# Loads of later tokens and of the first gate-up weights issued behind named stores of packed queries and keys

## The chip, the core and the metric

The kernel runs on one core of a Trainium2 chip. TensorE multiplies matrices, VectorE (DVE in the profile), ScalarE (ACT) and GpSimd (POOL) work on tiles, and SyncE (SP) does nothing here but issue DMA transfers. The transfers that SyncE issues go into one queue, whose packets are spread over 16 DMA engines. The metric is the device time of one execution in microseconds; of several runs the median counts.

## What is computed

A layer norm of 2048 tokens of width 448 feeds two branches, and both are added to the input. One is causal attention with 16 heads of width 28 inside four blocks of 512 tokens, with a memory of the earlier blocks. The other is a gated feed-forward network with 1792 hidden columns.

```python
xn = _layernorm(x, axis=-1)
# attention, per block s of 512 tokens, 16 heads
logits = einsum("bhqd,bhkd->bhqk", qs, ks) * scale + mask
a_dot  = einsum("bhqk,bhkd->bhqd", softmax(logits), vs)
a_mem  = einsum("bhld,bhde->bhle", phi(qs), M) / (einsum("bhld,bhd->bhl", phi(qs), z)[..., None] + 1e-6)
o = g * a_mem + (1 - g) * a_dot          # g = sigmoid(beta)
M, z = M + phi(ks)^T vs, z + sum(phi(ks))
# feed-forward
h = sigmoid(xn @ w_gate) * (xn @ w_up)
return x + concat(o) @ wo + h @ w_down
```

## The kernel before

Every float32 operand of a large product is split into a high part and a low rest, and a product is a sum of eleven matmuls over the four slices of 128 rows that the width needs (the list TERMS).

The kernel has two stages. The front stage goes over the four blocks of 512 tokens. For block b it multiplies the values (`values`, L326 to L332), then runs a loop over seven packed tiles c of keys and queries, 128 columns each (`keys_queries`, L339 to L358). The keys fill the first 448 of the 896 packed columns and the queries the rest. Position k in the loop is c in the first three blocks. For each tile:

- TensorE makes pp (L344, eleven matmuls of 128x512).
- ScalarE copies it to the high half of the tile qk (L345), and makes e, the feature map of keys or queries, where it is needed (L349, L350).
- VectorE writes the low half of qk (L351).
- SyncE stores qk to the DRAM tensor qd, 512 KB (L352). For the queries of the second to fourth block it also stores e to the DRAM tensor fd (L357).

Between these, `key_rows` (L364, matmul pk, and the copy kn, L366) turns the keys of tile k - 2, and `update` (L372, matmul pmm) adds to the memory. `turn` (L95, matmul pt) turns the next block's normalised tokens into its operand. In a block after the second, `recall` (L390, matmul n) multiplies the memory with phi, which is read back from fd (`phi_queries`, L383).

The second stage runs the feed-forward network (`gated`) with attention in between, and then the output projection. TensorE is in its written order there too. The generator `ffn = gated()` is advanced a step at a time: its first step only calls `load_up(0)` (L178, a raw gate-up tile of 512 KB), and its second splits that tile (`ready_up(0)`), loads the next (`load_up(1)`, L178) and the first down tile (`load_down(0)`, L185, 224 KB). In the front stage these two steps are taken at k = 5 of the second and third block (L554). The further steps come in the last block.

What sets the order: in the front stage, TensorE, ScalarE and VectorE run their instructions in the order in which the program writes them. SyncE and GpSimd do not: the compiler's scheduler puts their instructions where it expects them to be ready. A load that depends on nothing can therefore stand far ahead of its place in the program. In before the loads of the third and fourth block's tokens (L528, tiles acc2 and acc3, 896 KB each), both raw gate-up tiles (L178) and the first down tile (L185) stand at the top of SyncE's queue, right behind the four small gate loads; only the store vd of the values (L332, 1024 KB) comes between. The first store of qk comes behind all of them.

The tag "4k" of the pool `mid` has four buffers. At the start two hold wv's raw halves and one holds the last raw tile of wqk. The tile qk of c = 0 takes the fourth, c = 1 and c = 2 take wv's, c = 3 takes the buffer of c = 0 once its store has landed, and c = 4 that of wqk's raw tile.

PSUM banks are shared likewise: pk of odd c and pmm of even i use one bank with the tag "pd", so the first pmm waits until the copy kn has emptied the second pk.

Of the kernel before, what the change touches and what calls it, by code (L numbers as in the profile page):

```python
# [9 lines left out]
F32 = mybir.dt.float32  # L10
# [6 lines left out]
P = 128  # L17
# [44 lines left out]
def kernel(  # L62
# [10 lines left out]
    nc = tc.nc  # L73
# [8 lines left out]
    acc = [keep.tile([P, NT, D], F32, name=f"acc{b}") for b in range(NB)]  # L82
# [25 lines left out]
    def x_block(b):  # L108
        return x[b * L:(b + 1) * L, :].rearrange("(t p) d -> p t d", p=P)
# [5 lines left out]
    def bank(name, tag):  # L115
        return ps.tile([P, L], F32, name=name, tag=tag, bufs=banks[tag])
# [17 lines left out]
    qd = [dram.tile([2 * D, 2, L], F32, name=f"qd{b}") for b in range(NB)]  # L134
# [9 lines left out]
    def four_k(dtype, name):  # L144
        return mid.tile([P, 2, L], dtype, name=name, tag="4k", bufs=4)
# [122 lines left out]
    with tc.tile_pool(name="front", bufs=2) as sb, tc.manual_schedule(engines=FRONT):  # L268
# [10 lines left out]
        def statistics(b, t0, steps):  # L279

            stats = sb.tile([P, steps, 6], F32, name=f"stats{steps}")
            mv = sb.tile([P, steps, 2], F32, name=f"mv{steps}")
            vh = sb.tile([P, steps], F32, name=f"vh{steps}")
            for t in range(steps):
                V.bn_stats(stats[:, t, :], acc[b][:, t0 + t, :])  # L285
                V.bn_aggr(mv[:, t, :], stats[:, t, :])
            V.tensor_scalar(vh, mv[:, :, 1], EPS, -0.5, op0=ALU.add, op1=ALU.mult)
            return mv, vh

        def root(vh):  # L290
            y = sb.tile([P, vh.shape[1]], F32, name=f"y{vh.shape[1]}")
            A.activation(y, vh, AF.Sqrt, scale=-2.0)
            return y
# [15 lines left out]
        def normalise(b, t, mean, y):  # L309
            xn = sb.tile([P, 512], F32, name="xn")  # L310
            V.tensor_scalar(xn[:, :D].rearrange("p (m h c) -> p h m c", h=H, c=4),
                              acc[b][:, t, :].rearrange("p (h m c) -> p h m c", h=H, c=4), mean, y,
                              op0=ALU.subtract, op1=ALU.mult)
            if b == 0:
                A.activation(xn[:, D:], xn[:, 384:D], AF.Copy)
            else:
                G.tensor_copy(xn[:, D:], xn[:, 384:D])
            return xn

        def turn(b, t, xn):  # L320
            transpose_split(bank("pt", "s"), xn, xs[b], t)
# [7 lines left out]
        def store_values(b, t, pv):  # L329
            A.activation(vst[:, t, :, :DH], pv[:, :D].rearrange("p (h d) -> p h d", d=DH), AF.Copy)  # L330
            if t == NT - 1:
                nc.sync.dma_start(vd[b], vst.rearrange("p t h d -> p t (h d)"))  # L332

        def values(b, t):
            pv = bank("pv", "p")
            value_terms(b, t, pv, EARLY[1] if b == 0 else TERMS)
            store_values(b, t, pv)

        def keys_queries(b, c):  # L339

            qk = four_k(F32R, "qk")
            pp = bank("pp", ("p", "gu" if b < NB - 1 else "s")[c % 2])
            for n, (a, w) in enumerate(TERMS):
                T.matmul(pp, wqk[c][:, w, :], xs[b][:, a, :], start=n == 0, stop=n == len(TERMS) - 1)  # L344
            A.activation(qk[:, 0, :], pp, AF.Copy)  # L345
            e = None
            if (c < 4 and b < NB - 1) or (c > 2 and b > 0):
                e = sb.tile([P, L], F32, name="e", tag="e", bufs=5)
                A.activation(e, pp, AF.Relu, scale=-1.0)  # L349
                A.activation(e, e, AF.Exp, scale=-1.0)  # L350
            V.tensor_sub(qk[:, 1, :], pp, qk[:, 0, :].bitcast(F32))  # L351
            nc.sync.dma_start(qd[b][c * P:(c + 1) * P], qk.bitcast(F32))  # L352
            if e is not None:
                V.scalar_tensor_tensor(e, pp, 0.0, e, op0=ALU.max, op1=ALU.add)
                if c > 2 and b > 0:
                    lo = max(c * P - D, 0)
                    nc.sync.dma_start(fd[b][lo:(c + 1) * P - D], e[D + lo - c * P:])  # L357
            return e  # L358
# [22 lines left out]
        def phi_queries(b, i):  # L381
            phi = sb.tile([GW, L], F32, name="phi", tag="e", bufs=5)
            nc.sync.dma_start(phi, fd[b][i * GW:(i + 1) * GW])  # L383
            return phi

        def recall(b, i, phi):
            ts = sb.tile([P, L], F32, name="ts", bufs=1)
            tb = sb.tile([P, L], F32, name="tb", bufs=2)
            n2 = bank("n2", ("m", "pd")[i % 2])
            T.matmul(n2, mst[b % 2][i], phi, start=True, stop=True)  # L390
            V.transpose(ts, n2)
            weigh(sb, ts, gate[:, i:i + 1], MEM_EPS)
            V.transpose(tb, ts)
            nc.gpsimd.dma_start(od[b][P * i:P * (i + 1)], tb)
# [28 lines left out]
        def split_qk(c):  # L423
            r = raw_qk[c].rearrange("p (c n) -> p c n", c=4)
            A.activation(wqk[c][:, 0:4, :], r, AF.Copy)
            G.tensor_sub(wqk[c][:, 4:8, :], r, wqk[c][:, 0:4, :].bitcast(F32))
# [65 lines left out]
        ffn = gated()  # L492
        for b in range(NB):
            last = b == NB - 1
            phi, xn = {}, {}
            if b > 1:
                phi = {i: phi_queries(b - 1, i) for i in range(NG)}
            st = None
            for t in range(3 if b == 0 else 0, NT):
                values(b, t)  # L500
                if b > 1 and t > 0:
                    recall(b - 1, t - 1, phi[t - 1])
                if b == 0:
                    split_qk(t)
                if last:
                    continue
                if t == (3 if b == 0 else 0):
                    mv, vh = statistics(b + 1, 0, NT)
                if t == (3 if b == 0 else 0):
                    st = mv, vh, root(vh)  # L510
                if t == (3 if b == 0 else 2):
                    A.activation(one, ident[:, 0:1], AF.Exp)  # L512
            if st and b > 0:
                st = rstd(*st)
                for n in range(2):
                    xn[n] = normalise(b + 1, n, *st[n])
            e = {}
            for k, c in enumerate((3, 4, 5, 6, 0, 1, 2) if last else range(7)):
                e[c] = keys_queries(b, c)
                if b == 0 and c + 4 < 7:  # L520
                    split_qk(c + 4)
                if k == 0:
                    if b > 1:
                        recall(b - 1, NG - 1, phi[NG - 1])
                    if b == 0:
                        st = rstd(*st)
                    if b < 2:
                        nc.sync.dma_start(acc[b + 2], x_block(b + 2))  # L528
                    if b == 0:
                        A.activation(gate, gate, AF.Exp, scale=-1.0)  # L530
                        V.tensor_scalar_add(gate, gate, 1.0)
                        V.reciprocal(gate, gate)
                        V.tensor_scalar(gate_n, gate, -1.0, 1.0, op0=ALU.mult, op1=ALU.add)
                if last:
                    if k > 0:
                        next(ffn)
                    if 2 <= k < 6:
                        phi[k - 2] = phi_queries(b, k - 2)
                    if k > 4:
                        begin[k - 5]()  # L540
                        recall(b, k - 5, phi[k - 5])
                    continue
                if 2 <= k < 6:
                    key_rows(k - 2, e[k - 2])
                if 4 <= k:
                    update(b, k - 4)
                if k == 6:
                    update(b, 3)
                n = k - 1 if b == 0 else k + 1
                if 2 <= n < 6:  # L550
                    turn(b + 1, n - 2, xn[n - 2])
                if 0 <= n < 4 and n not in xn:
                    xn[n] = normalise(b + 1, n, *st[n])
                if b in (1, 2) and k == 5:  # L554
                    next(ffn)
            if last:
                for i in range(2):
                    for _ in range(FILLS[i]):
                        next(ffn)
                    if i == 0:  # L560
                        begin[2]()
                    recall(b, i + 2, phi[i + 2])
# [207 lines left out]
    with tc.manual_schedule(engines=MANUAL):  # L770
        next(steps)
        k = sum(FILLS) + 6
# [46 lines left out]
```

## Time and profile before

| what | value |
|---|---|
| three runs | 696.43, 697.25, 699.18 us |
| median | 697.25 us |
| span of the profiled execution | 697.6 us |
| DMA packets | 45797, 84.37 MB |
| mean granted TensorE clock | 0.997 of full |

The profiled execution is one execution of its own, and its span goes from its first to its last instruction; the profile gives no other time for it.

How to read it: a row of the timeline gives start and length in us from the span's start, the engine, the line of the program, the work as output <- inputs, how many instructions are merged, and in brackets the idle time of the engine before it with what ended it. A "q" behind an engine's name is its instruction queue, which issues DMAs. PEld is the weight load of a matmul, which overlaps the matmul before it. A row of the windows gives, for one stretch, the busy time of each engine and, as its last three numbers, the granted TensorE clock, the mean busy share of the DMA engines, and GB/s. A piece of the chain that reads "DMA qd<-qk" goes from the issue of a store to its landing.

### The profile page before, as it was taken

Reading aid. Unit: us, or ns where it says so; the run is one execution under the profiler, and the core shown is the slowest. Engines: PE = TensorE matmul, PEld = TensorE weight load, DVE = VectorE, ACT = ScalarE, POOL = GpSimd, SP = SyncE. Lnnn points to the kernel's source line nnn. Section 1 sums busy time; section 2 is a strip of 40 time slices with the busy share of each in tenths; the row PEclk is TensorE's granted clock in tenths of the full one; section 3 lists DMA queues with packets and bytes.
Section 4 is the critical chain, followed back from the end, with each engine's and each line's share of the span. In section 5 each row is a group of like instructions: output and inputs, shape, how many; then the busy total and the mean of one; then the engine's idle time right before and its main releaser. Section 6 shows DMA issues by size and latency. Waiting matters only on the chain.

```text
span 697.6 us, 10438 instructions
## 1 busy us (share of the span) xinstructions
PE 690.0 (99%) x3594; PEld 567.7 (81%) x3594; DVE 570.2 (82%) x994; ACT 343.6 (49%) x563; POOL 148.5 (21%) x349
## 2 busy tenths in 40 slices
PE   8989999999999999999999999999999999999997
PEld 7878878777878787877878778787787878778897
DVE  6665687658789898988898889998898889889863
ACT  5646646344455455543655446455644555446320
POOL 4400010101222131322222222132221322222000
PEclk9999999999999999999999999999999999999999
DMA  7833545687222423234323343324242432333342
GB/s 265 320 130 149 201 185 211 226 300 224 70 77 65 120 86 85 48 113 108 78 58 96 70 128 66 98 56 114 74 108 66 95 70 60 86 94 88 91 152 105
DMA packets 45797, 84.37 MB, mean 121 GB/s; under 512 B 6321, under 2 KB 20401, under 8 KB 45233
## 3 DMA queue, kind: packets, MB, share of 16 engines
q1 hardware_dynamic: 42736, 76.37, 35.3%
q0 software_dynamic: 3008, 7.34, 5.2%
q8 instruction: 28, 0.46, 0.3%
q14 instruction: 25, 0.20, 0.1%
HBM read 51.05 MB, written 32.64 MB: 120 GB/s over the span
## 4 chain that ended last, share of the span: by engine, by line
PE 94%; DMA 2%; DVE 1%; ACT 1%; SPq 0%; issue 0%; ACTq 0%
PE pgu L240 42%; PE pd L166 20%; PE pp L344 9%; PE st L597 5%; PE pa L672 5%; PE po L756 5%; PE pv L326 4%; PE pmm L372 2%; PE n L390 1%; DMA qd<-qk 1%; DMA acc<-in_x 1%; PE pt L95 1%; PE pk L364 1%; DVE stats L285 0%; ACT L512 0%
## 5 line engine op out<-in xcount | busy, mean ns | idle before, releaser
L240 PE MATMUL pgu<-xs,wgu 128*128 128x512 f32 x1232 | 321.0, 398 | 0.0
L240 PEld LDWEIGHTS pgu<-xs,wgu 128*128 128x128 f32 x1232 | 226.6, 188 | 48.0 <-issue 3.2
L166 PE MATMUL pd<-wdn,hh 128*128 128x448 f32 x672 | 162.4, 368 | 0.0
L612 POOL TENSOR_SCALAR_AFFINE_SELECT w<-w 128x256 f32<-128x256 f32 (+1 forms) x160 | 81.7, 512 | 254.1 <-ACT w L601 215.1
L166 PEld LDWEIGHTS pd<-wdn,hh 128*128 128x128 f32 x672 | 123.2, 188 | 15.1 <-issue 1.0
L652 ACT ACTIVATE w<-w 128x1024 f32<-128x1024 f32 (+1 forms) x96 | 87.1, 915 | 87.6 <-DVE w L651 87.0
L651 DVE TENSOR_TENSOR w<-w,mb 128x1024 f32<-128x1024 f32 (+1 forms) x96 | 99.7, 1049 | 0.2
L601 ACT ACTIVATE w<-st 128x512 f32<-128x512 f32 x128 | 75.0, 588 | 43.6 <-PE st L597 43.5
L614 DVE TRANSPOSE_TENSOR_REDUCE mx<-w 128x32 f32<-128x1024 f32 x64 | 79.1, 1235 | 12.7 <-POOL w L612 12.7
L344 PE MATMUL pp<-xs,wqk 128*128 128x512 f32 x308 | 80.6, 412 | 0.0
L344 PEld LDWEIGHTS pp<-xs,wqk 128*128 128x128 f32 x308 | 58.1, 192 | 14.8 <-issue 2.4
L169 DVE TENSOR_TENSOR acc<-pd,acc 128x448 f32<-128x448 f32 x112 | 67.4, 602 | 2.7 <-PE pd L166 2.5
L597 PE MATMUL st<-qk 84*128 84x128 f32 (+3 forms) x256 | 64.0, 311 | 0.0
L251 ACT ACTIVATE hh<-sg 128x512 fp32r<-128x512 f32 x56 | 35.1, 627 | 44.5 <-DVE sg L249 35.0
L597 PEld LDWEIGHTS st<-qk 84*128 84x128 f32 x256 | 48.4, 189 | 8.6 <-ACT w L601 0.2
L248 ACT ACTIVATE sg<-pgu 128x512 f32<-128x512 f32 x56 | 33.3, 594 | 40.1 <-PE pgu L240 40.1
L641 DVE STREAM_TRANSPOSE mb<-top 128x1024 f32<-128x1024 f32 x32 | 39.8, 1242 | 10.3 <-POOL top L638 10.1
L351 DVE TENSOR_TENSOR qk<-pp,qk 128x512 fp32r<-128x512 f32 x28 | 19.3, 688 | 34.6 <-ACT e L349 27.3
L249 DVE SCALAR_TENSOR_TENSOR sg<-sg,pgu 128x512 f32<-128x512 f32 x56 | 37.4, 668 | 4.8 <-PE pgu L240 4.8
L252 DVE SCALAR_TENSOR_TENSOR hh<-sg,hh 128x512 fp32r<-128x512 f32 x56 | 38.6, 690 | 2.7 <-ACT hh L251 2.5
L326 PE MATMUL pv<-wv,xs 128*128 128x448 f32 x176 | 39.7, 377 | 0.3
L672 PE MATMUL pa<-w,vv 128*32 128x128 f32 (+3 forms) x512 | 38.4, 436 | 0.0
(100 smaller groups left out, 639.2 us busy)
## 6 DMA issues: line engine op xcount, KB each, us to landing
qk<-qd SPq DMA_DIRECT2D x192, 112.0 KB
qd<-qk SPq DMA_DIRECT2D x28, 512.0 KB
raw<-in_w_ffn SPq DMA_DIRECT2D x14, 512.0 KB
vd<-vst SPq DMA_DIRECT2D x4, 1024.0 KB
vv<-vd SPq DMA_DIRECT2D x16, 256.0 KB
od<-w POOLq DMA_DIRECT2D x16, 256.0 KB, 4.0
sums<-od SPq DMA_DIRECT2D x32, 128.0 KB
out<-acc SPq DMA_DIRECT2D x16, 224.0 KB
```

Source lines behind the costliest of these rows:

```text
L166: T.matmul(pd[:, :D], l, r, start=n == 0, stop=n == len(mms) - 1)
L169: V.tensor_add(acc[b][:, t, :], pd[:, :D], acc[b][:, t, :])
L240: T.matmul(dst, wgu[f][:, w, side * P:(side + 1) * P], xs[b][:, a, :], start=n == 0, stop=n == len(TERMS) - 1)
L326: T.matmul(pv[:, :D], xs[b][:, a, t * P:(t + 1) * P], wv[w], start=n == 0, stop=n == len(TERMS) - 1)
L344: T.matmul(pp, wqk[c][:, w, :], xs[b][:, a, :], start=n == 0, stop=n == len(TERMS) - 1)
L597: T.matmul(st[:, at:at + L - kb * P], self.qk[:KS, 1, h, kb * P:(kb + 1) * P], self.qk[:KS, 0, h, kb * P:], start=True, stop=True)
L601: A.activation(w, st, AF.Copy)
L612: G.affine_select(d, d, pattern=pattern, base=0, channel_multiplier=-1, compare_op=ALU.is_ge, fill=MASK)
L614: V.tensor_reduce(mx[:, 16 * (n - 1):16 * (n + 1)], w3[:, n // 2, :2 * L].rearrange("p (b n) -> p b n", n=32), axis=mybir.AxisListType.X, ...
L651: V.tensor_sub(w, w, m)
L652: A.activation(w, w, AF.Exp, scale=SCALE)
L672: T.matmul(pa[32 * j:32 * j + 32, kb * P:], self.vv[:, kb, 32 * j:32 * j + 32], self.pairs[j // 2].block(j % 2, kb), start=kb == 0, stop=k ...
```

## The change

Each store of qk is kept by name. The load of the third and fourth block's tokens moves in the program from k = 0 to k = 3 of the loop, and it may now not be issued before the store of that same tile. The two steps of the feed-forward generator at k = 5 stay, but the DMAs that they issue on SyncE may not go out before the store of that tile. The rule only orders instructions of SyncE: a load behind a store waits for the store's issue, not for its landing.

```diff
+        stored = {}
+
         def keys_queries(b, c):
...
-            nc.sync.dma_start(qd[b][c * P:(c + 1) * P], qk.bitcast(F32))
+            stored[b, c] = nc.sync.dma_start(qd[b][c * P:(c + 1) * P], qk.bitcast(F32)).ins
...
-                    if b < 2:
-                        nc.sync.dma_start(acc[b + 2], x_block(b + 2))
...
+                if b < 2 and k == 3:
+                    with tc.issue_after(stored[b, c]):
+                        nc.sync.dma_start(acc[b + 2], x_block(b + 2))
                 if b in (1, 2) and k == 5:
-                    next(ffn)
+                    with tc.issue_after(stored[b, c]):
+                        next(ffn)
```

SyncE's queue in the front stage, in the order of issue (block numbers from 0, c from 0):

```
before                                   after
x, wv, wqk, gate loads                   x, wv, wqk, gate loads
acc2, acc3, raw up 0, raw up 1           vd of block 0
vd of block 0                            qd of block 0, c = 0 to 3
raw down 0                               acc2
qd of block 0, c = 0 to 6                qd of block 0, c = 4 to 6
vd, qd and fd of block 1, c = 0 to 5     vd of block 1, qd c = 0 to 3, fd c = 3
first phi of block 1                     acc3
qd and fd of block 1, c = 6              qd and fd of block 1, c = 4, 5
three phi of block 1                     raw up 0
vd, qd and fd of block 2, c = 0 to 5     qd and fd of block 1, c = 6
raw down 1                               four phi of block 1
first phi of block 2                     vd, qd and fd of block 2, c = 0 to 5
qd and fd of block 2, c = 6              raw up 1, raw down 0
three phi of block 2                     qd and fd of block 2, c = 6
                                         two phi of block 2, raw down 1, two phi
```

From the fourth block on both queues are the same, and so is the order on the other four engines.

## The prediction

> **What bounds the kernel now.** I read the page first: the span, the busy rows and the chain of work that ended last.
>
> ```profile
> span 697.6 us, 10438 instructions
> PE 690.0 (99%) x3594; PEld 567.7 (81%) x3594; DVE 570.2 (82%) x994; ACT 343.6 (49%) x563; POOL 148.5 (21%) x349
> PE 94%; DMA 2%; DVE 1%; ACT 1%; SPq 0%; issue 0%; ACTq 0%
> ```
>
> TensorE is busy for 690.0 of 697.6 us and carries 94% of the chain. A transfer is therefore worth only the time for which TensorE stands still because of it. The 2% of the chain put down to DMA asks where that is, so next I read TensorE's timeline of the first block (columns: start, length, engine, line, work; in brackets the idle time before it and what ended it).
>
> ```profile
> 27.92 2.81 PE L344 MATMUL pp<-xs,wqk 128*128 128x512 f32 x11
> ...
> 34.00 0.60 PE L364 MATMUL pk<-ident,e 128*128 128x128 f32 x4
> 36.73 1.13 PE L372 MATMUL pmm<-vst,kn 128*112 128x128 f32 x8 [2.14 <-ACT kn L366]
> ...
> 38.05 4.37 PE L344 MATMUL pp<-xs,wqk 128*128 128x512 f32 x11
> 42.26 0.60 PE L364 MATMUL pk<-ident,e 128*128 128x128 f32 x4
> ...
> 43.92 2.80 PE L344 MATMUL pp<-xs,wqk 128*128 128x512 f32 x11
> 46.56 1.91 PE L372 MATMUL pmm<-vst,kn 128*112 128x128 f32 x16
> ```
>
> One step of the loop over the packed tiles runs from a pk to where the next would stand. The step at 34.00 ends at 42.26, after 8.26 us. The step after it, with the same instructions, ends at 46.56, after 4.30 us. So 8.26 - 4.30 = 3.96 us are lost here: 2.14 us idle, 4.37 - 2.80 = 1.57 us in a slow pp, and 0.25 us of slower small pieces. The chain and ScalarE's timeline name the cause, and the windows the granted clock (third last column) with the DMA share and GB/s behind it.
>
> ```profile
> 25.08 9.27 DMA qd<-qk
> ```
>
> ```profile
> 34.45 0.60 ACT L345 ACTIVATE qk<-pp 128x512 fp32r<-128x512 f32 x1 [3.87 <-DMA qd<-qk]
> ...
> 36.10 0.58 ACT L366 ACTIVATE kn<-pk 128x512 f32<-128x512 f32 x1
> ```
>
> ```profile
> 0.00:10.00 10.00, 8.37 (x42) 7.71 (x43) 5.08 (x17) 4.87 (x12) 3.22 (x12) 1.00 0.76 237
> 10.00:20.00 10.00, 9.73 (x50) 8.18 (x49) 8.19 (x25) 5.51 (x13) 5.21 (x5) 1.00 0.70 254
> 28.00:30.00 2.00, 2.00 (x11) 1.64 (x10) 2.00 (x4) 1.97 (x4) 1.37 (x2) 1.00 1.00 410
> 38.00:40.00 2.00, 2.00 (x8) 1.63 (x7) 1.93 (x5) 0.74 (x2) 0.24 (x1) 0.54 0.20 78
> 40.00:42.00 2.00, 2.00 (x7) 1.56 (x6) 0.81 (x2) 0.00 (x0) 0.24 (x1) 0.61 0.65 262
> ```
>
> The first tile's store is issued at 25.08 and lands 9.27 us later, at 34.35. The fourth tile takes that store's buffer, so ScalarE stands for 3.87 us, its kn copy comes at 36.10, and that copy frees the PSUM bank for pmm. The clock then fell to 0.54 and 0.61 of full. The store is slow because the DMA engines are full (share 1.00, 410 GB/s) with what SyncE issued ahead of it:
>
> ```profile
> 13.23 1.09 SPq L528 DMA_DIRECT2D acc<-in_x  x2
> 16.26 4.32 SPq L178 DMA_DIRECT2D raw<-in_w_ffn  x2
> 20.70 0.65 SPq L332 DMA_DIRECT2D vd<-vst  x1
> 21.39 0.74 SPq L185 DMA_DIRECT2D rawd<-in_w_ffn  x1
> ```
>
> These five loads are two of 896 KB, two of 512 KB and one of 224 KB: 3040 KB, or 3.11 MB, that nothing needs yet. At 410 GB/s they take 7.6 us.
>
> **The change, part by part.** No instruction is added or removed. TensorE, VectorE, ScalarE and GpSimd keep their order exactly. Only SyncE's queue is rearranged.
>
> First edit: acc[2] goes behind the first block's fourth store and acc[3] behind the second block's fourth. Second edit: the first raw gate-up load goes behind the second block's sixth store. The next one, with the first down load, goes behind the third block's sixth.
>
> *The gain.* The loads left ahead of the first store are x's first two blocks, wv, and wqk: 1792 + 896 + 1792 KB = 4.59 MB. In before, 2.37 + 2.54 = 4.91 MB had moved by 20.00, so their work ends by about 20 us. Then come vd (1.05 MB, issued at 20.70) and the first store (0.52 MB, at 25.08). At 410 GB/s vd takes 2.6 us and is gone before 25.08. The store then has 1.3 us of work and perhaps 2 us of latency, estimated from the 2.9 us that an fd store takes further down. That is about 28.4. ScalarE can use the buffer when the fourth pp ends, at 27.92 + 2.81 = 30.73, so 2.3 us are to spare. The wait goes, TensorE does not stop, and the step costs 4.30 us: -3.96. Bounds: -2.4 if the slow stretch stays, -3.96 if all goes. I take all, as the slow pp directly follows the idle time and pp is 2.80 in the next step.
>
> *The loads at their new places.* acc[2] is issued at about 33 us and needs 0.92 MB / 410 = 2.2 us behind one store; VectorE reads it first at 50.49 - 3.96 = 46.5. That hides it with some 8 us, and acc[3] in the next block likewise. The first raw tile is issued at about 80 on the old scale and read at 116.22. All three cost 0; if the cover were gone, TensorE would wait behind the statistics.
>
> ```profile
> 50.49 0.63 DVE L285 BATCH_NORM_STATS2 stats<-acc 128x6 f32<-128x448 f32 x1
> ```
>
> ```profile
> 116.22 1.05 ACT L85 ACTIVATE wgu<-raw 128x1024 fp32r<-128x1024 f32 x1
> ```
>
> *What is late next.* The queue shifts at two more places. At the end of the second and third blocks SyncE also loads phi (queries after the feature map) for the matmul n. In before the first phi of each block goes out ahead of the seventh tile's two stores (qd, then fd). In after all four go behind both. So the first phi takes the second's old place. Here are the issues, the windows and TensorE's weight loads for n, times on the old scale:
>
> ```profile
> 80.08 0.46 SPq L383 DMA_DIRECT2D phi<-fd  x1
> 82.80 0.34 SPq L352 DMA_DIRECT2D qd<-qk  x1
> 83.46 0.32 SPq L357 DMA_DIRECT2D fd<-e  x1
> 83.87 3.27 SPq L383 DMA_DIRECT2D phi<-fd  x3
> ```
>
> ```profile
> 86.35 0.79 SPq L383 DMA_DIRECT2D phi<-fd  x2
> ```
>
> ```profile
> 86.72 0.39 PEld L390 LDWEIGHTS n<-phi,mst 112*128 112x128 f32 x2
> ```
>
> And the same for the third block:
>
> ```profile
> 116.80 0.32 SPq L357 DMA_DIRECT2D fd<-e  x1
> 118.56 0.33 SPq L185 DMA_DIRECT2D raw<-in_w_ffn  x1
> 119.06 1.17 SPq L383 DMA_DIRECT2D phi<-fd  x1
> 120.33 0.38 SPq L352 DMA_DIRECT2D qd<-qk  x1
> 120.75 0.42 SPq L357 DMA_DIRECT2D fd<-e  x1
> 121.45 4.01 SPq L383 DMA_DIRECT2D phi<-fd  x3
> ```
>
> ```profile
> 122.00:123.00 1.00, 1.00 (x7) 0.94 (x6) 0.00 (x0) 0.55 (x1) 0.00 (x0) 1.00 1.05 426
> 123.00:124.00 1.00, 1.00 (x7) 0.93 (x6) 0.00 (x0) 0.00 (x0) 0.00 (x0) 1.00 1.01 387
> 124.00:125.00 1.00, 1.00 (x5) 0.51 (x4) 0.00 (x0) 0.54 (x1) 0.00 (x0) 1.00 0.53 203
> ```
>
> ```profile
> 123.94 0.39 PEld L390 LDWEIGHTS n<-phi,mst 112*128 112x128 f32 x2
> ```
>
> Second block: the third phi waits for the fd store issued at 83.46 and goes out at 86.35, so a small transfer lands 2.9 us after issue. The phi issued at 83.87 then lands near 86.8 to 87.1, and n wants it at 86.72. Bounds 0 and 0.4 us; I take 0.2.
>
> Third block: 426 + 387 + 203 KB = 1.02 MB move from 122 to 125, which is exactly the qd store (0.52), the fd store (0.26) and the phi behind them (0.23). That phi's data end at about 124.5. It lands 0.3 to 0.7 us later, at 124.8 to 125.2, and n wants it at 123.94. So with the second's timing the first phi costs up to 1.3 us. In after SyncE is free earlier (the phi at 119.06 held it for 1.17 us, so the qd store goes out some 0.3 us sooner), but the engines are fuller: raw and down, 0.75 MB issued behind the sixth tile's fd store of 116.80, stand ahead of the stores, where the raw load at 118.56 and a phi, 0.46 MB, stood. The other bound is 0. I take 0.8, nearer the row of the second phi. Both waits sit on TensorE and nothing later takes them back.
>
> *The sum* against the profiled execution: -3.96 + 0.2 + 0.8 = -2.96, a span of 697.6 - 2.96 = 694.6 us. The median of the runs shown, 697.25, lies 0.35 below that span, so the time is 694.3 us.
>
> [...]
>
> **The rivals.**
>
> *The key loads hide.* Both phis land in time, the price of 1.0 falls away, and the time is 697.25 - 3.96 = 693.3. For it: in before the first phi, issued at 80.08, had over 6 us until 86.72, and the bounds reach 0. Against it: the place in the queue above. Chance 0.25.
>
> *The slow stretch is not won back in the median.* [...] If the middle run had none, only 2.4 us are won and 1.0 paid: 697.25 - 1.4 = 695.9. Chance 0.11.
>
> *Not faster: the third block's phi comes so late that the clock falls again.* One wait in front of n at 123.94. A stall of 2.14 us or more would draw the same 1.57 us of slow clock. If the phi lands at 127.0, the cost is 3.06 + 1.57 + 0.2 = 4.83 against 3.96 won: 697.25 + 0.9 = 698.1. It decides once the phi lands after about 126.1, where the stall of 2.14 makes cost and gain equal; each us later is a us slower. For it: the 0.75 MB of weights now ahead of the stores, 1.8 us of work at 410 GB/s. Against: that work starts at about 119 and is nearly over when the qd store comes. Chance 0.08; over 700.7 about 0.03.
>
> *The wait stays.* If the first store lands after 30.73 all the same, because vd rather than the loads holds it up, the fourth tile still waits and the time is about 696.7. Against: vd's 2.6 us fit before 25.08. Chance 0.05.
>
> **How the numbers follow.** The forecast, 694.3, has 0.50, with its own range 693.5 to 695.2; 0.01 is left for the unknown. The range of 692.9 to 696.6 takes in the hidden key loads and the unrecovered clock, and leaves out the two last cases and the tails. About 0.5%, or 3.5 us, is what a measurement of this kernel can tell from no change. Below 693.8 lie the hidden loads (most of 0.25) and about 0.18 of the forecast: faster 0.42. Slower 0.04. Same 0.54.
>
> **What would show it.** ScalarE's fourth qk near 30.8 with no DMA before it; the step from the third pk near 4.3 us; granted clock 1.00 from 38 to 42; acc loads after the fourth stores. Then idle time of TensorE in front of the first n of the third block (near 120 on the new scale), about 0.8 us, and of the second (near 83), about 0.2. I am wrong if the stall at 34 remains, if n's wait is over 1.3 us, or if VectorE waits for acc.

## The result and the profile after

The changed kernel is a little slower, not faster.

| kernel | runs | median, us | lowest to highest |
|---|---|---|---|
| before | 20 | 697.25 | 695.67 to 700.35 |
| changed | 20 | 698.79 | 698.03 to 700.65 |

The ratio is 1.0023, with a 95% interval of 1.0013 to 1.0034. The forecast was 694.3 us, in a range of 692.9 to 696.6.

The page of the changed kernel gives a span 0.9 us shorter than that of before, although its runs are longer. The two profiles alone would therefore have given the wrong sign.

```profile
span 696.7 us, 10437 instructions
...
PE 687.8 (99%) x3594; PEld 565.1 (81%) x3594; DVE 570.2 (82%) x994; ACT 343.9 (49%) x563; POOL 148.7 (21%) x349
...
PE 95%; DMA 2%; DVE 1%; ACT 0%; SPq 0%; issue 0%
```

The time of this profiled execution is known: 698.46 us, which is 1.8 us over its span, and in the 20 runs the time lies 1.6 to 1.8 us over the span. By that distance the profiled execution of before, span 697.6, took about 699.3 us (an estimate). It was one of the longer ones of its kernel, not one near the median.

First the place where before lost its time. These are TensorE's timeline and ScalarE's in the changed kernel:

```profile
33.91 0.60 PE L366 MATMUL pk<-ident,e 128*128 128x128 f32 x4
34.35 1.04 PE L374 MATMUL pmm<-vst,kn 128*112 128x128 f32 x8
...
35.58 2.81 PE L346 MATMUL pp<-xs,wqk 128*128 128x512 f32 x11
38.23 0.60 PE L366 MATMUL pk<-ident,e 128*128 128x128 f32 x4
```

```profile
30.68 0.60 ACT L347 ACTIVATE qk<-pp 128x512 fp32r<-128x512 f32 x1 [0.19 <-PE pp L346]
```

The wait for the store is gone: the fourth qk starts at 30.68 and follows its matmuls. The step from the third pk takes 38.23 - 33.91 = 4.32 us, where it took 8.26.

Now the first n of the second and of the third block, and the longest of TensorE's waits (who waited for whom: us in total, times, longest):

```profile
83.79 1.10 PE L392 MATMUL n<-phi,mst 112*128 112x512 f32 x2 [0.74 <-DMA phi<-fd]
...
123.18 1.10 PE L392 MATMUL n<-phi,mst 112*128 112x512 f32 x2 [1.94 <-DMA phi<-fd]
```

```profile
PE n L392 <- DMA phi<-fd: 2.7, 2, 1.9
PE warm L433 <- POOL ident masks.py:199: 1.5, 1, 1.5
PE pt L95 <- DVE xn L311: 0.7, 1, 0.7
```

Before had no wait in front of n. Now two of them leave TensorE idle for 2.7 us. They are at the places that the forecast named, and longer than it said: 0.74 and 1.94 where it had 0.2 and 0.8.

### The profile page after: what moved, and what is told of

The parts are those of the page before. It is cut to its first block, busy times and chain, and to the rows that moved or that the text cites. A ratio compares the mean times of both kernels' runs of the same rounds, so it can differ in the third digit from the quotient of the medians.

```text
span 696.7 us, 10437 instructions
## 1 busy us (share of the span) xinstructions
PE 687.8 (99%) x3594; PEld 565.1 (81%) x3594; DVE 570.2 (82%) x994; ACT 343.9 (49%) x563; POOL 148.7 (21%) x349
## 4 chain that ended last, share of the span: by engine, by line
PE 95%; DMA 2%; DVE 1%; ACT 0%; SPq 0%; issue 0%
PE pgu L240 42%; PE pd L166 20%; PE pp L346 10%; PE st L601 5%; PE pa L676 5%; PE po L760 5%; PE pv L326 3%; PE n L392 2%; DMA phi<-fd 1%; DMA acc<-in_x 1%; PE pmm L374 1%; PE pt L95 1%; PE pk L366 1%; DVE qk L353 0%; DVE e L356 0%; ACT qk L347 0%
## 5 line engine op out<-in xcount | busy, mean ns | idle before, releaser
L346 PE MATMUL pp<-xs,wqk 128*128 128x512 f32 x308 | 79.0, 405 | 0.0
```

## The experiments

Theory A is that the change takes away a stop of TensorE worth about 2 us in the first block, and pays some 3 us in front of n. Its rivals blame something else for the cost. All kernels but the three of the third group were timed in interleaved rounds with the kernel before; those three were profiled and timed once.

### Before again, and each edit alone

**Before again.** No edit.

> The kernel before, unchanged, for a second profile. Theory A (the stop of TensorE in the first block costs about 2.4 us in a usual execution, and the slow clock of another 1.6 us follows it in some executions only): the wait of ScalarE for the first store and TensorE's idle time of about 2.1 us are there again, but the granted clock from 38 to 42 us is 1.00 and the span is 695.5 to 696.0 us instead of 697.6. Theory B (the slow clock belongs to every execution): clock near 0.55 again, span near 697.6. Theory C (the first profile had an unusually long wait): TensorE idle for clearly less than 2.1 us. Time 697.1 in all of them.

697.81 us in 12 runs, ratio 1.0014 (1.0002 to 1.0026) for the same kernel. So the interval of such a comparison can miss by about 0.15%, and the 0.23% of the result should be read with that in mind; why the two differ is not known. The profiled execution took 700.11 us. TensorE was idle for 2.82 us, and a slow stretch followed as in the first profile: the pt took 1.06 us instead of 0.60 and the pp 3.99 instead of 2.80, at a mean clock of 0.997. Theory A expected it at full clock; that was a miss, and it needed another profile, further down. The runs say more. Each comes with its mean granted clock. Of the 65 runs of before that stand beside the kernels of this group and the next, 14 have a clock of 0.998 or less, with a median of 699.65 us; the other 51 have a median of 697.11. In the repeat itself it is 3 of 12.

**The first edit alone.** The second one is undone:

```diff
                 if b in (1, 2) and k == 5:
-                    with tc.issue_after(stored[b, c]):
-                        next(ffn)
+                    next(ffn)
```

> The first edit alone: the loads of the third and fourth block's tokens behind the fourth stores, the feed-forward loads at the top of the queue as before. 1.28 MB instead of 3.11 MB then stand ahead of the first store, which should land 1.83 MB / 410 GB/s = 4.5 us earlier, at about 29.9, before the 30.73 at which ScalarE can use the buffer. The first phi of the second and third block goes out ahead of the seventh tile's stores, as in before. Theory A (the change wins 2.4 us in the first block and loses 3 us in front of the first n of two blocks): 697.1 - 2.4 = 694.7 us, no wait for phi. Rival (the new waits in front of n come from the token loads, not from where phi stands in the queue): waits of 0.7 and 1.9 us stay and the time is 698.4.

695.52 us, ratio 0.9971 (0.9957 to 0.9986). All 11 runs lie between 695.41 and 695.68, all with a clock of 0.999 or more. TensorE waits for no transfer, so the rival falls: moving the token loads costs nothing and is enough to remove the wait.

**The second edit alone.** The token loads are back at k = 0 without a tie:

```diff
+                    if b < 2:
+                        nc.sync.dma_start(acc[b + 2], x_block(b + 2))
...
-                if b < 2 and k == 3:
-                    with tc.issue_after(stored[b, c]):
-                        nc.sync.dma_start(acc[b + 2], x_block(b + 2))
```

> The second edit alone: the feed-forward loads behind the sixth stores, the token loads at the top of the queue as before. 1.84 MB stand ahead of the first store, which lands about 3.1 us earlier, near 31.2; ScalarE waits about 0.5 us and TensorE not at all. All four phi stand behind the seventh tile's stores, as in the changed kernel. Theory A: waits in front of n of about 0.7 and 1.9 us and the time of the changed kernel, 698.4 to 698.8. Rival (phi waits come from the token loads): no waits, 694.7.

699.95 us in 6 runs, 698.29 to 700.95; ratio 1.0040 (1.0021 to 1.0058). That is over the 698.4 to 698.8 expected, but four of the six have a clock of 0.998 or less; the other two took 698.29 and 699.09 us. The first block is free of the wait here too, and the 0.5 us expected of ScalarE did not come either. The waits in front of n are back. From TensorE's waits:

```profile
PE n L392 <- DMA phi<-fd: 2.4, 2, 1.7
```

So either edit alone cures the first block, and the cost belongs to the second edit.

**The weight loads earlier.** The changed kernel with one word changed:

```diff
-                    with tc.issue_after(stored[b, c]):
+                    with tc.issue_after(stored[b, 0]):
                         next(ffn)
```

> The changed kernel with one difference: the feed-forward loads are tied to the first store of their block instead of the sixth, so they go out early in the second and third block and the first phi again stands ahead of the seventh tile's stores. Theory A: no wait in the first block and none in front of n, so 2.4 us less than before, 694.7 us, and about 3.7 us less than the changed kernel. Rival (anything else in the change costs the time, such as DMA contention from moving loads into the second and third block): it stays above 697.

695.51 us, ratio 0.9966 (0.9951 to 0.9981), 11 runs from 695.39 to 695.84. Not the 694.7 expected, for the median of before holds less to win than 2.4 us: 697.29 - 695.51 = 1.8 us in this group. This kernel and the first edit alone beat both kernels. Its first n, of the second and of the third block, with no wait:

```profile
82.85 1.02 PE L392 MATMUL n<-phi,mst 112*128 112x512 f32 x2
...
120.07 1.02 PE L392 MATMUL n<-phi,mst 112*128 112x512 f32 x2
```

Against it the changed kernel's first n stand 0.94 us later in the second block and 3.11 us later in the third, so the third block adds 2.17 us. The two waits cost 0.2 us more each than the idle time of 0.74 and 1.94 us that the trace puts in front of them.

### The place of phi, or the loads ahead of it

**Phi held behind the stores, weight loads early.** The kernel just above, with phi tied to the seventh tile's fd store:

```diff
-                    nc.sync.dma_start(fd[b][lo:(c + 1) * P - D], e[D + lo - c * P:])
+                    stored["f", b, c] = nc.sync.dma_start(fd[b][lo:(c + 1) * P - D], e[D + lo - c * P:]).ins
...
+            if ("f", b, 6) in stored:
+                with tc.issue_after(stored["f", b, 6]):
+                    nc.sync.dma_start(phi, fd[b][i * GW:(i + 1) * GW])
+            else:
+                nc.sync.dma_start(phi, fd[b][i * GW:(i + 1) * GW])
```

> The kernel with the weight loads early (695.5 us, no wait), with one difference: all phi loads of the second and third block are tied behind the seventh tile's fd store, the place that they have in the changed kernel, with no weight loads ahead of those stores but the small down load in the third block. Theory P (the place behind the two stores alone makes the phi late): waits in front of n as in the changed kernel, 0.7 and 1.9 us, time 698.4 or more. Theory D (the weight loads ahead in the queue make it late): no waits, 695.5. Both together (the forecast's sizes): about 0.3 in the second block and 0.5 to 1.2 in the third, time 696.3 to 697.0.

697.05 us, 12 runs from 696.70 to 697.64, so 1.5 us over the kernel without the tie. Its first n:

```profile
83.54 1.10 PE L396 MATMUL n<-phi,mst 112*128 112x512 f32 x2 [0.31 <-DMA phi<-fd]
...
121.86 1.10 PE L396 MATMUL n<-phi,mst 112*128 112x512 f32 x2 [0.87 <-DMA phi<-fd]
```

The place, with no more weights ahead of it than in before (the small down load of the third block), gives waits of 0.31 and 0.87, about the forecast's 0.2 and 0.8. With the weight loads ahead in the queue they are 0.74 and 1.94. Neither theory alone holds: each part is about half of the price.

**Only the third block's loads late, and only the second's.** The tie of the changed kernel is kept in one block and set to the first store in the other:

```diff
-                    with tc.issue_after(stored[b, c]):
+                    with tc.issue_after(stored[b, c if b == 2 else 0]):
```

> The changed kernel with the first raw gate-up load early in the second block; the loads of the third block stay behind the sixth store. Only the wait in the third block is left: 1.9 us of idle time, the first n 2.1 us late, so 697.6 us in executions with full clock. If the slow clock is drawn by this wait, about half of the executions are some 2 us longer again, with a granted clock of 0.998 or less, as in the changed kernel; if by the smaller wait of the second block, none.

698.71 us, 12 runs. Six lie from 697.12 to 698.29 at a clock of 0.999 or more, and six from 699.13 to 699.78 at 0.997. The median of the first six is 697.6, as expected, and half of the executions have the longer time. The one wait in the profile is 2.31 us, in an execution at full clock.

The second kernel has `b == 1` in the same line.

> The opposite: the loads of the third block early, the first raw load of the second block behind the sixth store. Only the wait of 0.7 us is left, with the first n 0.9 us late: 696.4 us. If the slow clock needs the long wait, every execution has a granted clock of 0.999 or more and the times spread by no more than 0.5 us.

696.51 us, 12 runs from 695.96 to 696.96, all with a clock of 0.999 or more. Its profiled execution has 0.34 us of idle time there, so this wait varies, and the runs spread by 1.0 us, not the 0.5 expected. The trace names an instruction of VectorE (mv, which ends at 83.32) as its end, not phi. That is hardly the cause: with the weight loads earlier the same n starts at 82.85, and mv ends at 83.35 there. Together the two kernels show that the wait of about 2 us draws the half-speed stretch, in half of the executions, and the short one does not.

**Phi first, weight loads where the change has them.** The seventh tile's qd store is tied behind the first phi, which is moved into the loop ahead of it:

```diff
-            stored[b, c] = nc.sync.dma_start(qd[b][c * P:(c + 1) * P], qk.bitcast(F32)).ins
+            with ExitStack() as order:
+                if c == 6 and b in (1, 2):
+                    order.enter_context(tc.issue_after(stored["phi", b, 0]))
+                stored[b, c] = nc.sync.dma_start(qd[b][c * P:(c + 1) * P], qk.bitcast(F32)).ins
...
-            nc.sync.dma_start(phi, fd[b][i * GW:(i + 1) * GW])
+            stored["phi", b, i] = nc.sync.dma_start(phi, fd[b][i * GW:(i + 1) * GW]).ins
...
-                phi = {i: phi_queries(b - 1, i) for i in range(NG)}
+                phi = {i: early[b - 1] if i == 0 else phi_queries(b - 1, i) for i in range(NG)}
...
+                if b in (1, 2) and k == 6:
+                    early[b] = phi_queries(b, 0)
                 e[c] = keys_queries(b, c)
```

> The changed kernel with the weight loads where they are, behind the sixth store, but the seventh tile's qd store tied behind the first phi, which so goes out ahead of the two stores. In the second block the raw load is still ahead of the phi. If the place of phi is what matters, no waits in front of n and 695.5 us; if the token or weight loads cost time in another way, more.

695.65 us, ratio 0.9972 (0.9958 to 0.9986), 12 runs from 695.49 to 695.97. The waits are gone although the weight loads are as late as in the change. In the second block phi still stands behind the raw load. In the third the scheduler put it even ahead of the sixth tile's stores, so there it also stands ahead of the weight loads. The second block alone therefore shows that the place matters with the weights where they are.

### Profiles of the same kernels in other executions

**Before, two more.** No edit.

> The kernel before once more, for a profile of an execution with full clock. So far both its profiles fell on executions with the slow clock (spans 697.6 and 698.4), which about 14 of 65 executions are. Theory A: with full clock the span is 695 to 696 us, TensorE's idle time before the first pmm is 1.2 to 2.0 us, the step from the third pk to where the next stands is 4.3 us plus that idle time and some 0.2 us, and the granted clock from 38 to 42 us is 1.00. Rival: the step costs 8.3 us again with the clock at 1.00, and the executions differ elsewhere.

> As the one before it, in case that one falls on the slow clock: the same numbers. Of the two, the execution with the longer idle time before the first pmm should be the longer one, by that difference.

Both executions had full clock: 697.65 and 697.0 us, spans 695.9 and 695.3. TensorE's timeline of the first, then of the second:

```profile
33.87 0.60 PE L364 MATMUL pk<-ident,e 128*128 128x128 f32 x4
36.42 1.13 PE L372 MATMUL pmm<-vst,kn 128*112 128x128 f32 x8 [1.95 <-ACT kn L366]
...
37.74 2.80 PE L344 MATMUL pp<-xs,wqk 128*128 128x512 f32 x11
40.38 0.60 PE L364 MATMUL pk<-ident,e 128*128 128x128 f32 x4
```

```profile
34.15 0.60 PE L364 MATMUL pk<-ident,e 128*128 128x128 f32 x4
35.98 1.13 PE L372 MATMUL pmm<-vst,kn 128*112 128x128 f32 x8 [1.23 <-ACT kn L366]
...
37.30 2.81 PE L344 MATMUL pp<-xs,wqk 128*128 128x512 f32 x11
39.95 0.60 PE L364 MATMUL pk<-ident,e 128*128 128x128 f32 x4
```

The idle time is 1.95 and 1.23 us and the pp after it takes its normal 2.80. The steps take 6.51 and 5.80 us, so against 4.30 they lose 2.2 and 1.5 us, not 3.96. Theory A holds: without the stretch the stop costs its idle time and 0.3 us. The first has 0.72 us more idle time and took 0.65 us longer, as expected.

**The changed kernel again.** No edit.

> The changed kernel, unchanged, for a second profile. About half of its executions have the slow clock. If this one has it (time near 700.2), Theory A says that the clock falls to half for 3.4 us within 4 us of the idle time in front of the third block's first n, that the matmuls there take about 1.7 us more, and that there is no slow stretch anywhere else before the end. If it has full clock, span 696.3 to 697.1 and waits of about 0.7 and 1.9 us. Rival: a slow stretch somewhere else in the span.

700.21 us, span 698.5. Its waits are those of the other profile (1.79 us here in the third block), but this execution has the stretch. TensorE's timeline, and the windows with the granted clock third from the end:

```profile
123.11 1.54 PE L392 MATMUL n<-phi,mst 112*128 112x512 f32 x2 [1.79 <-DMA phi<-fd]
123.66 4.36 PE L326 MATMUL pv<-wv,xs 128*128 128x448 f32 x11
```

```profile
122.00:124.00 2.00, 0.90 (x3) 0.61 (x3) 0.00 (x0) 0.00 (x0) 0.00 (x0) 0.90 0.74 220
124.00:126.00 2.00, 2.00 (x6) 1.38 (x5) 1.21 (x4) 0.00 (x0) 0.00 (x0) 0.50 0.36 114
126.00:128.00 2.00, 2.00 (x9) 1.82 (x8) 1.33 (x2) 0.00 (x0) 0.34 (x1) 0.74 0.00 0
```

The eleven pv after the wait take 4.36 us instead of 2.78. The clock lost is (0.10 + 0.50 + 0.26) x 2 = 1.7 us, which is 3.4 us at half speed, right behind the idle time. The windows from 38 to 42, 120 to 122 and 128 to 130 show 1.00, and the mean clock of the execution, 0.997, means 2.1 us lost in 698.5, so these 1.7 are most of it.

## Why the prediction was wrong

**The wait that goes.** The mechanism was right: too many bytes ahead of the first store, and a wait that vanishes when they go. The size was wrong, and it is the first step that failed: -3.96, read from one profiled execution and set against the median. The prediction tied the two by "the median of the runs shown, 697.25, lies 0.35 below that span". A run's time is 1.7 us above its span, so that execution stood 2 us above the median, and those 2 us were mostly the half-speed stretch that only 14 of 65 executions have. What the median had to win is 697.29 - 695.51 = 1.8 us. Even the lower bound of 2.4 was more than a stop without the stretch costs, 2.2 and 1.5 us in the two profiles. The rival "the slow stretch is not won back in the median" had this mechanism, with a chance of 0.11 and 2.4 us of gain; a sign of it was there to be read in the runs from 696.43 to 699.18.

**What is late next.** Place and cause were right: phi behind the seventh tile's stores, waits in front of the first n of two blocks, nothing later that takes them back. The size was not. Taken as 0.2 + 0.8 = 1.0 us, it is 698.46 - 695.51 = 2.95 us, where 698.46 is the median of the 11 runs of the changed kernel at a clock of 0.999 or more. The place costs 1.5 us of it. The other half comes from the weight loads. The forecast saw them ("the engines are fuller") and gave them no price: its upper bounds, 0.4 and 1.3, are the place alone, and its reason against more was that "that work starts at about 119 and is nearly over when the qd store comes". The issues and the windows of the third block in the changed kernel show that this step failed:

```profile
113.08 0.32 SPq L354 DMA_DIRECT2D qd<-qk  x1
113.74 0.32 SPq L359 DMA_DIRECT2D fd<-e  x1
114.11 0.63 SPq L178 DMA_DIRECT2D raw<-in_w_ffn  x1
114.79 1.03 SPq L185 DMA_DIRECT2D rawd<-in_w_ffn  x1
116.95 0.33 SPq L354 DMA_DIRECT2D qd<-qk  x1
117.61 0.33 SPq L359 DMA_DIRECT2D fd<-e  x1
118.05 1.57 SPq L385 DMA_DIRECT2D phi<-fd  x2
```

```profile
113.00:114.00 1.00, 1.00 (x6) 0.77 (x6) 0.96 (x4) 1.00 (x2) 0.00 (x0) 1.00 0.14 53
114.00:115.00 1.00, 1.00 (x6) 0.81 (x5) 0.99 (x2) 0.21 (x1) 0.00 (x0) 1.00 1.01 393
115.00:116.00 1.00, 1.00 (x11) 1.00 (x10) 0.47 (x1) 0.88 (x2) 0.00 (x0) 1.00 1.04 328
116.00:117.00 1.00, 1.00 (x10) 0.98 (x9) 0.77 (x2) 0.83 (x2) 0.00 (x0) 1.00 0.88 279
117.00:118.00 1.00, 1.00 (x7) 0.93 (x6) 0.96 (x3) 0.00 (x0) 0.00 (x0) 1.00 1.01 379
118.00:119.00 1.00, 1.00 (x7) 0.94 (x6) 0.60 (x3) 0.00 (x0) 0.00 (x0) 1.00 1.04 418
119.00:120.00 1.00, 1.00 (x7) 0.94 (x6) 0.00 (x0) 0.55 (x1) 0.00 (x0) 1.00 1.00 381
120.00:121.00 1.00, 1.00 (x7) 0.82 (x5) 0.00 (x0) 0.00 (x0) 0.00 (x0) 1.00 0.98 332
121.00:122.00 1.00, 0.24 (x2) 0.00 (x0) 0.00 (x0) 0.55 (x1) 0.00 (x0) 1.00 1.01 327
```

The sixth tile's two stores (0.52 and 0.26 MB, issued at 113.08 and 113.74) and the weights behind them (0.75 MB) make up 1.54 MB. By 117 the rows add up to 53 + 393 + 328 + 279 KB = 1.05 MB. So some 0.49 MB of it were still to move when the qd store was issued at 116.95. The DMA engines are full or nearly so from 114 to 122 (0.88 and more), at 279 to 418 GB/s, 355 in the mean, where the forecast priced the weights at 410. The first phi is issued at 118.05 and its n starts at 123.18, 5 us later. How much of these 5 us the transfers issued right behind this phi take (the second phi and a down load) was not tested.

**The clock again.** The rival in which the new wait draws a half-speed stretch asked for a stall of 2.14 us or more, with phi landing after 126. The stretch came at waits under 2 us already (1.79 in the profile that has it): 9 of the 20 runs have a clock of 0.998 or less, with a median of 700.27, so 1.8 us over the others. Because that is just under half of the runs, it lifts the median by only 698.79 - 698.46 = 0.3 us.

The sum, in the median, is -1.8 + 2.95 + 0.3 = +1.5 us, against +1.54 measured. These terms are differences of medians that follow on one another, so they must add up. What tests the 2.95 is the traces, with delays of 0.94 + 2.17 = 3.1 us, and the two kernels with one wait each, at full clock 696.51 and 697.6: 1.0 + 2.1 us over 695.51. The forecast had a stretch that is not won back and a stretch that is drawn anew as rivals, each by itself, and its bounds for the two waits end at 1.7 us. A small gain together with a large price stood nowhere in it, which is why the range ended at 696.6.

**The rest.** No engine waits longer for the token loads or the raw tiles at their new places, as forecast: VectorE 4.0 us for tokens and GpSimd 2.5 us for a raw tile, in both kernels. The first edit alone, at 695.52, shows it for the tokens, and the kernel with phi first, at 695.65, for the weights: their price falls on phi alone. The rival in which the wait stays has fallen. What the forecast said the profile would show was there: the fourth qk at 30.7, a step of 4.3 us, a clock of 1.00 from 38 to 42, and the two waits. So was one of its signs of being wrong, a wait of n over 1.3 us: it is 1.94. The two sizes of the sum were off, one by half and one by a factor of three, and the stretch was at the wrong place in it.

## What to carry to other kernels

Before a gain is read from a profile, the profiled execution must be placed among the runs, by its own time or by its span plus the usual distance and by its mean clock; a stall that is followed by a half-speed stretch has to be priced by how often the stretch comes. When a load is moved on an in-order queue, list which small, urgent transfers now stand behind it, and price the bytes ahead at the rate of the rows at that place. Here it was enough to move the token loads alone, or, with both groups moved, to tie the weights to an earlier store.

## What was not expected of the hardware

Idle time of TensorE of about 2 us draws a stretch of 3.4 us at half clock in some executions. In the first profile of before it comes behind 2.14 us of idle time and goes from 38.16 to 41.57, at a granted clock of 0.50. Counted by a mean clock of 0.998 or less, such executions are 14 of 65 runs of before and 3 of the 12 of its repeat, 9 of 20 of the changed kernel, 4 of 6 with the second edit alone, and 6 of 12 of the kernel with only the third block's wait. In the two kernels whose profiles show waits of 0.87 us and less none of 24 runs has it, nor any of the 34 runs of the three kernels without such a wait. The kernels without the wait also spread far less: 0.3 to 0.5 us, where the kernel before spreads by 4.7 in 20 runs.

The length of the stop alone does not decide it. The slow stretch followed in the three profiles with stops in front of pmm or n of 2.14, 2.82 and 1.79 us, and did not in the six where the longest such stop was 2.31, 1.95, 1.94, 1.67, 1.23 and 0.87 us. What else decides it was not shown.
